# One decode step on one core: 32x32 block transposes on VectorE in place of TensorE transposes, wide matmuls, and loads in another order and in longer runs

## The chip, the core and the metric

The kernel runs on 1 core of one Trainium2 chip. The metric is the device time of one execution in microseconds (us), the median of several runs. The profile is that of one execution. Engines: PE is TensorE (PEld its weight loads), DVE is VectorE, ACT is ScalarE, POOL is GpSimd, SP is SyncE, which here only issues DMAs.

## The reference, cut to what matters

One token goes through an attention branch over a window of cached keys and values and through an MLP branch; both read the same normalised vector and both are added to x.

```python
W = min(4096, max(256, Sk // 4))          # 4096 of Sk = 65536
xn = _layernorm(A_x)                      # 1 x 1024, bf16
q = (xn @ wq)                             # wq 1024 x 4096: 32 heads of 128
k, v = last W rows of k_cache, v_cache    # 4 groups of 4096 x 128, 8 heads each
p = softmax(q k^T * 128 ** -0.5)
a = (p @ v) @ wo                          # wo 4096 x 1024
y = _layernorm(xn)
m = gelu(y @ w1 + b1) @ w2 + b2           # w1 1024 x 3584, w2 3584 x 1024
return A_x + a + m
```

All of it is read once: wq 8.4 MB, w1 7.3, K 4.2, V 4.2, w2 7.3, wo 8.4, together 39.8 MB.

## The kernel before, in words

Everything is placed by hand, with semaphores between the engines; there are no loops on the chip, so each engine runs its instructions in program order. SP issues all large loads, in this order: wq and w1 (line 139, `load_rows`), K (line 187), V (line 192), and, once h is computed (the wait at line 286 stands between), w2 and wo (line 139 again). Each load fills the 128 partitions; one run of a partition is as long as its share of the load, 16 KB for a chunk of two rows of wq, 8 KB for a group of K. w2 goes into the space of w1, wo into that of wq. wo's seven chunks (8, 8, 8, 4, 2, 1, 1 rows per partition) end with small ones. Small loads (x as a column, x and b2 as rows, b1 as columns) are issued by ACT; x as a column is 128 runs of 16 bytes.

- Normalisation: DVE, ACT and two small matmuls (lines 196 to 246) give XNTb (for q) and YTb (for h).
- q (`row_product`, line 255): for each of the 8 rows of wq in a partition, eight matmuls of 512 columns with a single weight column; q stands as one row in PSUM. DVE and ACT copy it out, 32 tiny matmuls (line 273) turn it into columns.
- h (line 255): the same with w1, seven matmuls a row; the copies are at lines 281 and 283, the 28 tiny transposes at line 305, bias and gelu at lines 310 to 326.
- K: 128 transposes of 128x128 on PE (line 344), copied from PSUM back into the K buffer by DVE (line 351) and ACT (line 356). Scores: 128 matmuls of 8 columns with a K block as weights (line 366).
- Softmax: maximum per head across partitions (lines 371 to 387), exponential on ACT (line 392), sums (line 395).
- P V: 128 matmuls of 128 columns (line 433), all of a group in one column group of the array. The result is divided by the sum (line 439) and folded into columns OT (lines 444, 448).
- Output: x and b2 (lines 418, 419), w2 and wo (`out_rows_mms`, line 409) accumulate into one PSUM bank; each row of a weight takes four matmuls of 256 columns, one for each of the four 32-column groups of the array. ACT copies the result (line 457), and ACT and SP store it in two halves.

The matmuls of line 409 wait chunk by chunk for the loads of w2 and wo.

Of the kernel before, what the change touches and what calls it, by code (L numbers as in the profile page):

```python
# [9 lines left out]
D = 1024  # L10
F = 3584
HQ = 32
HKV = 4
DH = 128
REP = HQ // HKV
SK = 65536
W = 4096
NBLK = W // 128
FC = F // 128
KC = D // 128  # L20
NQ = HQ * DH
WQ_CHUNKS = [2, 2, 2, 2]
W1_CHUNKS = [2, 2, 2, 2]
W2_CHUNKS = [9, 9, 8, 2]
WO_CHUNKS = [8, 8, 8, 4, 2, 1, 1]
PAD = 32
# [14 lines left out]
def bass_parallel_sum__sliding_block_cached__mixer_channel_mlp__decode_kernel(  # L41
# [23 lines left out]
    s_x, s_xrow, s_b1T, s_b2, s_out = (nc.alloc_semaphore(n) for n in ("s_x", "s_xrow", "s_b1T", "s_b2", "s_out"))  # L65
    s_out2 = nc.alloc_semaphore("s_out2")
# [16 lines left out]
    identb = sb("identb", [128, 128], bf16)  # L83
    identf = sb("identf", [128, 128], f32)
    onesf = sb("onesf", [128, 128], f32)
    E4 = sb("E4", [128, 4 * 128], bf16)
    XB = sb("XB", [128, KC], bf16)
    XBR = sb("XBR", [1, 2 * D], bf16)
# [8 lines left out]
    ROW = sb("ROW", [1, NQ], bf16)  # L97
    Qrow = ROW[:, 0:NQ]
    Hrow = ROW[:, 0:F]
    ORow = sb("ORow", [128, 256], bf16)  # L100
    QT = sb("QT", [128, HQ], bf16)
    B1T = sb("B1T", [128, FC], bf16)
    HT = sb("HT", [128, FC], f32)
    U2 = sb("U2", [128, FC], f32)
    GT = sb("GT", [128, FC + PAD], bf16)
    MXP = sb("MXP", [128, 32], f32)
    MX32 = sb("MX32", [32, 1], f32)
    DIAG = sb("DIAG", [32, 32], f32)
    NMB = sb("NMB", [128, 32], f32)
    Pb = sb("Pb", [128, HKV * NBLK * REP + PAD], bf16)  # L110
    SUMP = sb("SUMP", [128, 128], f32)
    REC = sb("REC", [128, 1], f32)
    ON = sb("ON", [128, DH], bf16)
    OT = sb("OT", [128, 32 + PAD], bf16)
    KV = sb("KV", [128, HKV * W + HKV * NBLK * DH], bf16)
    KT = KV[:, 0:HKV * W]
    V = KV[:, HKV * W: HKV * W + HKV * NBLK * DH]
    W1 = sb("W1", [128, KC * F], bf16)
    W2 = W1[:, 0:FC * D]
    WA = sb("WA", [128, KC * NQ], bf16)  # L120
# [15 lines left out]
    def load_rows(dst, src, chunks, width, semaphores):  # L136
        c0 = 0
        for j, n in enumerate(chunks):
            sp.dma_start(  # L139
                dst[:, c0 * width:(c0 + n) * width].rearrange("p (c n) -> p c n", c=n),  # L140
                src[:, c0:c0 + n, :],
            ).then_inc(semaphores[j], 16)
            c0 += n


    with nc.allow_non_contiguous_dma(reason="small loads"):
        act.dma_start(XB[:, :], x_col).then_inc(s_x, 16)
        act.dma_start(XBR[:, 0:D], x_row).then_inc(s_xrow, 16)
        act.dma_start(XBR[:, D:2 * D], b2_row).then_inc(s_b2, 16)
        act.dma_start(B1T[:, :], b1_T).then_inc(s_b1T, 16)  # L150

    C["onesf"] = POOL.mark(pool.memset(onesf[:, :], 1.0))
    POOL.mark(pool.memset(identb[:, :], 0.0))
    pool.wait_ge(POOL.sem, POOL.cnt)
    C["identb"] = POOL.mark(pool.affine_select(
        out=identb[:, :], in_=identb[:, :], pattern=[[-1, 128]], compare_op=ALU.not_equal,
        fill=1.0, base=0, channel_multiplier=1))
    POOL.mark(pool.memset(identf[:, :], 0.0))
    pool.wait_ge(POOL.sem, POOL.cnt)
    C["identf"] = POOL.mark(pool.affine_select(  # L160
        out=identf[:, :], in_=identf[:, :], pattern=[[-1, 128]], compare_op=ALU.not_equal,
        fill=1.0, base=0, channel_multiplier=1))
    POOL.mark(pool.memset(E4[:, :], 0.0))
    pool.wait_ge(POOL.sem, POOL.cnt)
    pool.wait_ge(POOL.sem, POOL.cnt)
    for g in range(HKV):

        POOL.mark(pool.affine_select(
            out=E4[32 * g:32 * g + REP, :].rearrange("p (q m) -> p q m", q=4),
            in_=E4[32 * g:32 * g + REP, :].rearrange("p (q m) -> p q m", q=4),  # L170
            pattern=[[1, 4], [-1, 128]], compare_op=ALU.not_equal, fill=1.0,
            base=32 * g, channel_multiplier=4))
        pool.wait_ge(POOL.sem, POOL.cnt)
    POOL.mark(pool.memset(SUMP[:, :], 1.0))
    pool.wait_ge(POOL.sem, POOL.cnt)
    POOL.mark(pool.memset(GT[:, FC:FC + PAD], 0.0))
    pool.wait_ge(POOL.sem, POOL.cnt)
    POOL.mark(pool.memset(OT[:, 32:32 + PAD], 0.0))
    pool.wait_ge(POOL.sem, POOL.cnt)
    POOL.mark(pool.memset(Pb[:, HKV * NBLK * REP:], 0.0))  # L180
    C["consts"] = POOL.cnt


    load_rows(WA, wq_p, WQ_CHUNKS, NQ, s_wq)
    load_rows(W1, w1_p, W1_CHUNKS, F, s_w1)
    for g in range(HKV):
        sp.dma_start(
            KT[:, g * W:(g + 1) * W],
            A_k_cache[0, g, SK - W:SK, :].rearrange("(m b) d -> m (b d)", m=128),
        ).then_inc(s_k[g], 16)  # L190
    for g in range(HKV):
        sp.dma_start(
            V[:, g * NBLK * DH:(g + 1) * NBLK * DH],
            A_v_cache[0, g, SK - W:SK, :].rearrange("(m b) d -> m (b d)", m=128),
        ).then_inc(s_v[g], 16)


    def stats(src, ms, veps):
        DVE.mark(dve.tensor_reduce(  # L199
            out=ms[:, 0:2], in_=PS[:, 7 * 512: 7 * 512 + 16].rearrange("p (a k) -> p a k", a=2),  # L200
            axis=AX.X, op=ALU.add))
        C["d_sum"] = DVE.cnt
        dve.wait_ge(DVE.sem, DVE.cnt)
        DVE.mark(dve.tensor_scalar(out=ms[:, 2:4], in0=ms[:, 0:2], scalar1=INV_D, scalar2=None, op0=ALU.mult))
        dve.wait_ge(DVE.sem, DVE.cnt)
        DVE.mark(dve.tensor_tensor(out=ms[:, 4:5], in0=ms[:, 2:3], in1=ms[:, 2:3], op=ALU.mult))
        dve.wait_ge(DVE.sem, DVE.cnt)
        C[veps] = DVE.mark(dve.scalar_tensor_tensor(
            out=ms[:, 5:6], in0=ms[:, 3:4], scalar=EPS, in1=ms[:, 4:5], op0=ALU.add, op1=ALU.subtract))

    dve.wait_ge(s_x, 16)
    DVE.mark(dve.tensor_copy(XT16[:, 0:8], XB[:, :]))
    dve.wait_ge(DVE.sem, DVE.cnt)
    C["xsq"] = DVE.mark(dve.tensor_tensor(out=XT16[:, 8:16], in0=XT16[:, 0:8], in1=XT16[:, 0:8], op=ALU.mult))  # L214

    pe.wait_ge(DVE.sem, C["xsq"])
    pe.wait_ge(POOL.sem, C["onesf"])
    C["sum1"] = PE.mark(pe.matmul(PS[:, 7 * 512: 7 * 512 + 16], lhsT=onesf[:, :], rhs=XT16[:, 0:16]))  # L218
    dve.wait_ge(PE.sem, C["sum1"])
    stats(XT16, msx, "veps1")  # L220
# [3 lines left out]
    DVE.mark(dve.reciprocal(out=msx[:, 7:8], in_=msx[:, 6:7]))  # L224
    dve.wait_ge(DVE.sem, DVE.cnt)
    DVE.mark(dve.tensor_scalar(out=XNT[:, :], in0=XT16[:, 0:8], scalar1=msx[:, 2:3], scalar2=msx[:, 7:8],  # L226
                               op0=ALU.subtract, op1=ALU.mult))
    dve.wait_ge(DVE.sem, DVE.cnt)
    C["xn"] = DVE.mark(dve.tensor_copy(XNTb[:, :], XNT[:, :]))
    dve.wait_ge(DVE.sem, DVE.cnt)  # L230
    DVE.mark(dve.tensor_copy(YT16[:, 0:8], XNTb[:, :]))  # L231
    dve.wait_ge(DVE.sem, DVE.cnt)
    C["ysq"] = DVE.mark(dve.tensor_tensor(out=YT16[:, 8:16], in0=YT16[:, 0:8], in1=YT16[:, 0:8], op=ALU.mult))
    pe.wait_ge(DVE.sem, C["ysq"])
    C["sum2"] = PE.mark(pe.matmul(PS[:, 7 * 512: 7 * 512 + 16], lhsT=onesf[:, :], rhs=YT16[:, 0:16]))  # L235
    dve.wait_ge(PE.sem, C["sum2"])
    stats(YT16, msy, "veps2")
# [5 lines left out]
    DVE.mark(dve.reciprocal(out=msy[:, 7:8], in_=msy[:, 6:7]))  # L243
    dve.wait_ge(DVE.sem, DVE.cnt)
    C["y"] = DVE.mark(dve.tensor_scalar(out=YTb[:, :], in0=YT16[:, 0:8], scalar1=msy[:, 2:3], scalar2=msy[:, 7:8],
                                        op0=ALU.subtract, op1=ALU.mult))


    def row_product(weights, chunks, width, semaphores, vec, tiles, name):
        k = 0  # L250
        for j, n in enumerate(chunks):
            pe.wait_ge(semaphores[j], 16)
            for _ in range(n):
                for t in range(tiles):
                    last = pe.matmul(  # L255
                        PS[0:1, t * 512:(t + 1) * 512], lhsT=vec[:, k:k + 1],
                        rhs=weights[:, k * width + t * 512: k * width + (t + 1) * 512],
                        start=(k == 0), stop=(k == KC - 1))
                k += 1
        C[name] = PE.mark(last)  # L260

    pe.wait_ge(DVE.sem, C["d_sum"])
    row_product(WA, WQ_CHUNKS, NQ, s_wq, XNTb, 8, "q")
    dve.wait_ge(PE.sem, C["q"])
    C["d_qrow"] = DVE.mark(dve.tensor_copy(Qrow[:, 0:2048], PS[0:1, 0:2048]))  # L265
# [228 lines left out]
```

## Time and profile before

| what | value |
|---|---|
| time before, median of 3 runs | 102.41 us (102.35 to 102.55) |
| span of the profiled execution, first to last instruction | 101.1 us |
| PE busy | 69.9 us (69%) |
| DVE busy | 21.4 us (21%) |
| ACT busy | 13.8 us (14%) |
| HBM read | 39.86 MB, 394 GB/s over the span |
| mean granted TensorE clock | 0.825 |

How to read the rows that follow. In a line of groups, after the engine and the operation come the tiles (out<-in), the shape, the count, then busy time and mean ns of one, then idle time just before and what ended it. In a timeline or a chain the first two columns are the start in us from the span's start and the duration. In a table of stretches the columns after the engines are the granted clock (1.00 is full speed), the share of time in which the DMA engines were busy, and GB/s; a packet is counted where it begins, so a share can pass 1.00. An engine named with q (SPq) is its DMA issues.

### The profile page before, as it was taken

What the parts mean: (1) busy time and instruction counts of PE and PEld (TensorE: products, weight loads), DVE (VectorE), ACT (ScalarE), POOL (GpSimd) and SP (SyncE); (2) the same over time, 40 slices, a digit from 0 to 9 for tenths busy, and PEclk for the clock granted to TensorE, in tenths of its full rate; (3) what the DMA queues carried; (4) which work ended last, traced back from release to release, by engine and by line L of the source; (5) the groups of instructions that cost most, each with busy time, mean ns of one, the idle gap of its engine ahead of it and who ended that gap; (6) DMA issues with size and microseconds to landing.
All of it is one profiled execution on the core that took longest, in us unless ns stands there. A gap on an engine that the chain in (4) does not pass through costs nothing.

```text
span 101.1 us, 1804 instructions
## 1 busy us (share of the span) xinstructions
PE 69.9 (69%) x825; PEld 42.9 (42%) x825; DVE 21.4 (21%) x46; ACT 13.8 (14%) x16; POOL 4.8 (5%) x18
## 2 busy tenths in 40 slices
PE   0002299999955999998599986556999944070780
PEld 0001232333314223332599975244999833040420
DVE  0003530000045000001885953456000100000000
ACT  0400060000042000001563750040000000000001
POOL 6740000000000000000000000000000000000000
PEclk9999999999997558999999998555559999555555
DMA  4899999999999999999999999999999999999920
GB/s 97 363 441 405 442 428 421 415 441 420 442 431 414 432 431 401 421 418 421 415 431 421 415 454 422 445 408 424 424 394 462 421 421 428 421 418 399 398 101 1
DMA packets 4194, 39.96 MB, mean 395 GB/s; under 512 B 726, under 2 KB 730, under 8 KB 1244
## 3 DMA queue, kind: packets, MB, share of 16 engines
q1 hardware_dynamic: 3892, 39.85, 94.0%
q8 instruction: 6, 0.10, 0.4%
q10 hardware_dynamic: 296, 0.01, 0.2%
HBM read 39.86 MB, written 0.00 MB: 394 GB/s over the span
## 4 chain that ended last, share of the span: by engine, by line
DMA 38%; PE 34%; SPq 20%; DVE 5%; issue 1%; ACT 1%
PE PS L255 31%; DMA WA<-in_A_wo_dram 30%; SPq L139 20%; DMA XB<-in_A_x_dram 8%; DVE ROW L265 2%; PE PS L273 1%; PE PS L218 1%; PE PS L235 1%; PE PS L409 0%; ACT ORow L457 0%; DVE XNT L226 0%; ACT msx L222 0%; DVE msx L199 0%; DVE msy L199 0%; DVE YT L231 0%
## 5 line engine op out<-in xcount | busy, mean ns | idle before, releaser
L255 PE MATMUL PS<-WA,XNTb 128*1 128x512 bf16 x64 | 16.7, 429 | 0.3 <-DVE msy L199 0.3
L255 PE MATMUL PS<-W,YTb 128*1 128x512 bf16 x56 | 15.2, 441 | 0.0
L409 PE MATMUL PS<-WA,OT 128*32 128x256 bf16 x128 | 7.3, 379 | 9.3 <-DMA WA<-in_A_wo_dram 9.3
L255 PEld LDWEIGHTS PS<-WA,XNTb 128*1 128x1 bf16 x64 | 5.8, 92 | 10.7 <-issue 3.9
L433 PE MATMUL PS<-KV,Pb 128*32 128x128 bf16 x128 | 9.3, 261 | 0.0
L409 PEld LDWEIGHTS PS<-WA,OT 128*32 128x32 bf16 x128 | 3.8, 123 | 12.9 <-DMA WA<-in_A_wo_dram 10.3
L255 PEld LDWEIGHTS PS<-W,YTb 128*1 128x1 bf16 x56 | 5.2, 94 | 9.5 <-issue 4.2
L433 PEld LDWEIGHTS PS<-KV,Pb 128*32 128x32 bf16 x128 | 9.2, 120 | 0.0
L344 PE MATMUL PS<-identb,KV 128*128 128x128 bf16 x128 | 7.5, 219 | 1.5 <-ACT ROW L281 1.5
L344 PEld LDWEIGHTS PS<-identb,KV 128*128 128x128 bf16 x128 | 7.2, 98 | 2.1 <-ACT ROW L281 2.0
L218 PE MATMUL PS<-XT,onesf 128*128 128x16 f32 x2 | 0.6, 386 | 8.8 <-DVE XT L214 8.8
L351 DVE COPY KV<-PS 128x1024 bf16<-128x1024 bf16 x10 | 6.3, 683 | 0.7 <-PE PS L344 0.7
L356 ACT ACTIVATE KV<-PS 128x1024 bf16<-128x1024 bf16 x6 | 5.8, 1018 | 1.9 <-PE PS L344 1.9
L265 DVE CAST ROW<-PS 1x2048 bf16<-1x2048 f32 x1 | 2.3, 2279 | 15.4 <-PE PS L255 15.4
L409 PE MATMUL PS<-W,GT 128*32 128x256 bf16 x112 | 4.8, 320 | 1.1 <-DMA W<-in_B_w_dram 1.1
L283 DVE CAST ROW<-PS 1x2048 bf16<-1x2048 f32 x1 | 2.3, 2279 | 14.9 <-PE PS L255 14.9
L457 ACT ACTIVATE ORow<-PS 128x256 bf16<-128x256 f32 x1 | 0.4, 383 | 31.0 <-PE PS L409 31.0
L409 PEld LDWEIGHTS PS<-W,GT 128*32 128x32 bf16 x112 | 3.5, 111 | 1.8 <-DVE PS L387 1.6
L218 PEld LDWEIGHTS PS<-XT,onesf 128*128 128x128 f32 x2 | 0.5, 313 | 8.8 <-DVE XT L214 8.8
L267 ACT ACTIVATE ROW<-PS 1x2048 bf16<-1x2048 f32 x1 | 1.9, 1866 | 14.4 <-PE PS L255 14.4
L281 ACT ACTIVATE ROW<-PS 1x1536 bf16<-1x1536 f32 x1 | 1.4, 1439 | 16.6 <-PE PS L255 16.6
L366 PE MATMUL PS<-QT,KV 128*128 128x8 bf16 x128 | 3.4, 166 | 0.4 <-DVE KV L351 0.4
(75 smaller groups left out, 34.5 us busy)
## 6 DMA issues: line engine op xcount, KB each, us to landing
WA<-in_A_wq_dram SPq DMA_DIRECT2D x4, 2048.0 KB, 14.2
W<-in_B_w_dram SPq DMA_DIRECT2D x4, 1792.0 KB, 29.9
WA<-in_A_wo_dram SPq DMA_DIRECT2D x3, 2048.0 KB, 38.4
W<-in_B_w_dram SPq DMA_DIRECT2D x2, 2304.0 KB, 21.6
KV<-in_A_k_cache_dram SPq DMA_DIRECT2D x4, 1024.0 KB, 39.3
KV<-in_A_v_cache_dram SPq DMA_DIRECT2D x4, 1024.0 KB, 34.1
W<-in_B_w_dram SPq DMA_DIRECT2D x1, 2048.0 KB, 28.8
WA<-in_A_wo_dram SPq DMA_DIRECT2D x1, 1024.0 KB, 42.3
```

The lines of the kernel that those rows point to most:

```text
L139: sp.dma_start(dst[:, c0 * width:(c0 + n) * width].rearrange("p (c n) -> p c n", c=n), src[:, c0:c0 + n, :],).then_inc(semaphores[j], 16)
L218: C["sum1"] = PE.mark(pe.matmul(PS[:, 7 * 512: 7 * 512 + 16], lhsT=onesf[:, :], rhs=XT16[:, 0:16]))
L255: last = pe.matmul(PS[0:1, t * 512:(t + 1) * 512], lhsT=vec[:, k:k + 1], rhs=weights[:, k * width + t * 512: k * width + (t + 1) * 512], s ...
L265: C["d_qrow"] = DVE.mark(dve.tensor_copy(Qrow[:, 0:2048], PS[0:1, 0:2048]))
L267: C["a_qrow"] = ACT.mark(act.activation(out=Qrow[:, 2048:4096], in_=PS[0:1, 2048:4096], func=ACTF.Copy))
L283: C["d_hrow"] = DVE.mark(dve.tensor_copy(Hrow[:, 1536:F], PS[0:1, 1536:F]))
L344: last = pe.matmul(PSb[:, o:o + 128], lhsT=KT[:, col + bb * 128: col + (bb + 1) * 128], rhs=identb[:, :], is_transpose=True)
L351: C["dkt"][u] = DVE.mark(dve.tensor_copy(KT[:, col + 1024 * s: col + 1024 * (s + 1)], PSb[:, bk * 1024:(bk + 1) * 1024]))
L356: C["akt"][u] = ACT.mark(act.activation(out=KT[:, col + 1024: col + 2048], in_=PSb[:, bk * 1024:(bk + 1) * 1024], func=ACTF.Copy))
L366: last = pe.matmul(PS[:, g * 256 + b * 8: g * 256 + (b + 1) * 8], lhsT=KT[:, g * W + b * 128: g * W + (b + 1) * 128], rhs=QT[:, g * 8:(g + ...
L409: ins = pe.matmul(acc(a), lhsT=vec[:, c:c + 32], rhs=weights[:, c * D + a * 256: c * D + (a + 1) * 256], start=False, stop=(c == stop_at))
L433: last = pe.matmul(PS[32 * g:32 * g + 32, 4 * 512:4 * 512 + DH], lhsT=Pb[:, i * REP:i * REP + 32], rhs=V[:, i * DH:(i + 1) * DH], start=(b ...
```

## The change

- Loads. wq and w1 come in two chunks of four rows instead of four of two, w2 in chunks of 18 and 10 rows (before 9, 9, 8, 2), wo in 16, 8, 4, 2, 1, 1 (before 8, 8, 8, 4, 2, 1, 1). The order is wq, K, w1, V; w2 follows when q is computed, into wq's space; wo follows when h is computed, its rows 0 to 27 into w1's space and 28 to 31 into K's. x, b2 and b1 are loaded as four rows each, onto partitions 0, 32, 64 and 96 (b2: 1, 33, 65, 97).
- q and h: four matmuls of 512 (448) columns for the four column groups, the weight column broadcast to 32 columns; the results lie on four blocks of 32 equal partitions. DVE transposes 32x32 blocks (`dve.transpose`) to turn x, q, h and P into columns; four matmuls with a selection matrix SELQ and four copies build QB, q in a block-diagonal form.
- K: four transposes in place on DVE, 128x4096 each; scores in 32 matmuls of 512 columns with QB as weights. P: one transpose and 16 copies.
- P V: 32 matmuls of 512 columns over all four groups at once, taking turns on the column groups; a mask GMASK keeps each head's own group.
- Output: w2 and rows 0 to 27 of wo in two matmuls of 512 columns a row with one weight column (`bulk`), on two column groups in one PSUM bank; x, b2 and rows 28 to 31 in four matmuls of 256 columns in another. DVE copies the first bank in four pieces (BULK) and adds it to the second; SP stores the result in one DMA.

The diff, cut to its core (added lines alone where a whole part is new):

```diff
-WQ_CHUNKS = [2, 2, 2, 2]
-W1_CHUNKS = [2, 2, 2, 2]
-W2_CHUNKS = [9, 9, 8, 2]
-WO_CHUNKS = [8, 8, 8, 4, 2, 1, 1]
+WQ_CHUNKS = [4, 4]
+W1_CHUNKS = [4, 4]
+W2_CHUNKS = [18, 10]
+WO_CHUNKS = [16, 8, 4, 2, 1, 1]
+WO_BULK = 28
...
     load_rows(WA, wq_p, WQ_CHUNKS, NQ, s_wq)
-    load_rows(W1, w1_p, W1_CHUNKS, F, s_w1)
     for g in range(HKV):
         sp.dma_start(
             KT[:, g * W:(g + 1) * W],
...
+    load_rows(W1, w1_p, W1_CHUNKS, F, s_w1)
     for g in range(HKV):
         sp.dma_start(
...
+        act.dma_start(XB4[0:128:32, :], x_rows).then_inc(s_x, 16)
+        act.dma_start(XB4[1:128:32, :], b2_rows).then_inc(s_b2, 16)
+        act.dma_start(B1R[0:128:32, :], b1_rows).then_inc(s_b1, 16)
...
+    def wide_product(weights, chunks, width, semaphores, vec, n, banks, name):
+        k = 0
+        for j, rows in enumerate(chunks):
+            pe.wait_ge(semaphores[j], 16)
+            for _ in range(rows):
+                for b in range(2):
+                    for a in range(4):
+                        lo = k * width + (2 * a + b) * n
+                        last = pe.matmul(
+                            PS[32 * a:32 * a + 32, banks[b] * 512: banks[b] * 512 + n],
+                            lhsT=vec[:, k:k + 1].to_broadcast([128, 32]), rhs=weights[:, lo:lo + n],
+                            start=(k == 0), stop=(k == KC - 1))
+                k += 1
+        C[name] = PE.mark(last)
+
+    wide_product(WA, WQ_CHUNKS, NQ, s_wq, XNTb, 512, [0, 1], "q")
+
+    sp.wait_ge(PE.sem, C["q"])
+    load_rows(WA, w2_p, W2_CHUNKS, D, s_w2)
...
+    C["TQ"] = d(dve.transpose(TQ[:, :], Q4[:, :]))
...
+    for g in range(HKV):
+        dve.wait_ge(s_k[g], 16)
+        C["kt"].append(d(dve.transpose(KT[:, g * W:(g + 1) * W], KT[:, g * W:(g + 1) * W])))
...
+        for hb in range(2):
+            for c in range(4):
+                last = pe.matmul(
+                    PS[32 * g:32 * g + 32, hb * 512:(hb + 1) * 512],
+                    lhsT=QB[:, (g * 4 + c) * 32:(g * 4 + c + 1) * 32], rhs=kg[:, c, 16 * hb:16 * hb + 16, :],
+                    start=(c == 0), stop=(c == 3))
...
+    d(dve.transpose(PT1[:, :], Pb[:, :]))
+    dw()
+    for g in range(HKV):
+        for a in range(4):
+            C["PT"] = d(dve.tensor_copy(
...
+    wide_product(W1, W1_CHUNKS, F, s_w1, YTb, QW // 2, [4, 5], "h")
+    sp.wait_ge(PE.sem, C["h"])
+    load_rows(W1, wo_p, WO_CHUNKS[:3], D, s_wo[:3])
+    load_rows(KT, wo_p, WO_CHUNKS[3:], D, s_wo[3:], first=WO_BULK)
...
+    for b in range(NB):
+        q = b % 4
+        last = pe.matmul(PS[32 * q:32 * q + 32, 3 * 512:4 * 512], lhsT=PT[:, b * 32:(b + 1) * 32], rhs=vb[:, b],
+                         start=(b < 4), stop=(b >= NB - 4))
...
+    def bulk(weights, vec, c, lo, first, last):
+        for q in range(2):
+            ins = pe.matmul(PS[32 * q:32 * q + 1, 6 * 512:7 * 512], lhsT=vec[:, c:c + 1],
+                            rhs=weights[:, lo + q * 512: lo + (q + 1) * 512], start=first, stop=last)
+        return ins
...
+            if c < WO_BULK:
+                last = bulk(W1, OT, c, c * D, False, c == WO_BULK - 1)
...
+            else:
+                for a in range(4):
+                    lo = (c - WO_BULK) * D + a * 256
+                    last = pe.matmul(PS[32 * a:32 * a + 32, 7 * 512:7 * 512 + 256],
+                                     lhsT=OT[:, c:c + 1].to_broadcast([128, 32]), rhs=KT[:, lo:lo + 256],
+                                     start=False, stop=(c == 31))
...
+    dve.wait_ge(PE.sem, C["bulk"])
+    for a in range(4):
+        q = a // 2
+        lo = 6 * 512 + (a % 2) * 256
+        d(dve.tensor_copy(BULK[32 * a:32 * a + 1, :], PS[32 * q:32 * q + 1, lo:lo + 256]))
+    dw()
+    dve.wait_ge(PE.sem, C["fin"])
+    C["out"] = d(dve.tensor_tensor(out=ORow[:, :], in0=bank(7, 0, 256), in1=BULK[:, :], op=ALU.add))
+    sp.wait_ge(DVE.sem, C["out"])
+    sp.dma_start(out_rows, ORow[0:128:32, :]).then_inc(s_out, 16)
```

More of the change, by code (lines that the diff above doesn't have):

```diff
@@ new lines, in bulk @@
+    def bulk(weights, vec, c, lo, first, last):
[3 more added lines that the diff above has]
+        return ins
+    pe.wait_ge(DVE.sem, C["GT"])
+    c = 0
+    for j, n in enumerate(W2_CHUNKS):
+        pe.wait_ge(s_w2[j], 16)
+        for _ in range(n):
+            bulk(WA, GT, c, c * D, c == 0, False)
+            c += 1
```

515 lines of the change are left out of this document (232 added, 283 removed).

## The prediction

> **What bounds the kernel now.** I read the page first (engines, DMA slices, queues), then the chain of waits in order of time, then busy time in stretches near the end, then the timeline of TensorE.
>
> ```profile
> span 101.1 us, 1804 instructions
> ...
> PE 69.9 (69%) x825; PEld 42.9 (42%) x825; DVE 21.4 (21%) x46; ACT 13.8 (14%) x16; POOL 4.8 (5%) x18
> ...
> DMA  4899999999999999999999999999999999999920
> ...
> DMA packets 4194, 39.96 MB, mean 395 GB/s; under 512 B 726, under 2 KB 730, under 8 KB 1244
> q1 hardware_dynamic: 3892, 39.85, 94.0%
> q8 instruction: 6, 0.10, 0.4%
> q10 hardware_dynamic: 296, 0.01, 0.2%
> ```
>
> The DMA engines are full from the second slice to the 38th. Queue q1 (the loads issued by SP) takes 94.0% of 16 engines' span: 95.1 us of 101.1. The bytes are the same after the change, so only three things can move the end: what a byte costs on the DMA engines, a hole in their stream, and the work behind the last landing.
>
> ```profile
> 0.73 7.63 DMA XB<-in_A_x_dram
> ...
> 67.91 30.42 DMA WA<-in_A_wo_dram
> 98.34 0.04 issue
> 98.38 0.43 PE PS L409 x4
> ...
> 98.84 0.38 ACT ORow L457
> ```
>
> The chain ends with the last row of wo: landed at 98.34, multiplied by 98.8, copied by 99.2, then the store. The chain names TensorE and SP earlier (lines 255 and 139), but the DMA slices are full there too: SP was only late with issues that stood far back in a full queue. So shorter TensorE stages are worth nothing by themselves.
>
> ```profile
> 78.00:91.00 13.00, 7.07 (x178) 5.45 (x172) 0.54 (x2) 0.00 (x0) 0.00 (x0) 0.82 1.01 425
> ...
> 95.00:96.00 1.00, 0.40 (x12) 0.14 (x8) 0.00 (x0) 0.00 (x0) 0.00 (x0) 0.50 1.00 385
> 96.00:97.00 1.00, 0.89 (x16) 0.32 (x8) 0.00 (x0) 0.00 (x0) 0.00 (x0) 0.50 0.50 188
> 97.00:98.00 1.00, 0.89 (x12) 0.25 (x12) 0.00 (x0) 0.00 (x0) 0.00 (x0) 0.50 0.27 100
> ```
>
> The last three columns are granted clock, DMA share and GB/s. Full engines move 425 GB/s in long runs (16 KB a partition) and 385 GB/s in 2 KB runs. Half of the engines are done by about 96.5, the last at about 98.
>
> **The change, part by part.** Times are positions in the profiled span of 101.1 us; the median of the runs shown, 102.41, lies 1.3 us above it, and I keep that distance.
>
> *Longer runs.* One engine moves 425/16 = 26.6 bytes/ns in 16 KB runs and 385/16 = 24.1 in 2 KB runs: 617 and 85 ns a run. The difference, 532 ns for 14,336 bytes, gives 26.9 bytes/ns and a fixed 9 ns a run. Before, the 27 large loads have 128 runs each, 8 for each engine: 216. After there are 20 loads (2 wq, 4 K, 2 w1, 4 V, 2 w2, 6 wo): 160. That saves 56 x 9 = 0.50 us. Each load also ends in one small completion packet per engine; they fit the count, 27 x (128 + 16) = 3888 of the 3892 packets of q1. Seven fewer at no more than 9 ns: 0.06 us. Bounds: 0, if runs above 16 KB are cut up again, and 0.6.
>
> *Small loads.* x and b1 go from 128 short runs each to 4 rows each. Queue q10 falls from 0.2% of the span to nearly nothing: 0.2 us per engine (0.15 to 0.25 by the rounding). The x load's 7.63 us at the start shrink too, but then q waits for wq: no gain.
>
> By the Trainium skill (DMA: Bandwidth & Descriptors, Anatomy of one DMA) each DMA carries about 2.0 us of fixed cost; seven fewer would then give 14 us if it stood in the stream. The trace disagrees: the share is 1.01 across many loads, so that cost is overlapped, and the sum doesn't take it.
>
> *Sum for the stream:* 0.50 + 0.06 + 0.20 = 0.76; the last landing comes at 98.34 - 0.76 = 97.58, if no hole opens.
>
> *Holes.* SP issues w2 behind q and wo behind h, past K and V, now issued earlier.
>
> ```profile
> 17.55 15.48 SPq L192 DMA_DIRECT2D KV<-in_A_v_cache_dram  x4
> ...
> 99.25 0.60 SPq L461 DMA_DIRECT2D out_dram<-ORow  x1
> ```
>
> SP got its last V load out at 33.0, when about 31 us x 425 GB/s = 13.2 of 24.1 MB had moved: some 11 MB can stand in the queue. By 425 GB/s from 2 us, wq has landed at 22, K at 32, w1 at 49, V at 59, w2 at 76. w2 must be issued by 59 and wo by 76.
>
> ```profile
> 12.53 16.66 PE L255 MATMUL PS<-WA,XNTb 128*1 128x512 bf16 x64 [0.27 <-DVE msy L199]
> ...
> 12.91 0.13 PEld L255 LDWEIGHTS PS<-WA,XNTb 128*1 128x1 bf16 x1 [0.30 <-issue]
> ...
> 17.60 0.13 PEld L255 LDWEIGHTS PS<-WA,XNTb 128*1 128x1 bf16 x1 [0.30 <-issue]
> 18.01 10.66 PEld L255 LDWEIGHTS PS<-WA,XNTb 128*1 128x1 bf16 x50 [0.29 <-issue]
> ...
> 32.52 15.17 PE L255 MATMUL PS<-W,YTb 128*1 128x512 bf16 x56
> ...
> 38.45 8.73 PEld L255 LDWEIGHTS PS<-W,YTb 128*1 128x1 bf16 x41 [0.30 <-issue]
> ...
> 62.33 1.23 DVE L371 TENSOR_REDUCE MXP<-PS 128x32 f32<-128x1024 f32 x1 [2.85 <-PE PS L366]
> ...
> 66.80 1.02 ACT L392 ACTIVATE Pb<-PS 128x1024 bf16<-128x1024 f32 x1 [7.20 <-DVE PS L387]
> ...
> 80.84 1.27 PE L409 MATMUL PS<-W,GT 128*32 128x256 bf16 x40
> ```
>
> From 12.91 to 17.60 are 12 loads, 0.427 us apart: 512 columns at half clock. From 18.01 on it is 10.66/50 = 0.213. Four column groups do overlap: 40 matmuls of 256 columns in 1.27 us are 32 ns each, where one alone would need 107. So the q product, 16 steps of four, has 8 steps left when wq ends: 22 + 8 x 0.427 = 25.8, and w2 follows at once. Copies, transposes and selection of q I put at 3.5 us, so the K transposes start at about 29.
>
> ```profile
> L351 DVE COPY KV<-PS 128x1024 bf16<-128x1024 bf16 x10 | 6.3, 683 | 0.7 <-PE PS L344 0.7
> L265 DVE CAST ROW<-PS 1x2048 bf16<-1x2048 f32 x1 | 2.3, 2279 | 15.4 <-PE PS L255 15.4
> L395 DVE TENSOR_REDUCE SUMP<-Pb 128x32 f32<-128x1024 bf16 x1 | 2.0, 1971 | 1.1 <-ACT Pb L392 1.1
> L387 DVE TENSOR_TENSOR PS<-PS,NMB 128x1024 f32<-128x1024 f32 x1 | 1.2, 1233 | 0.0
> ```
>
> No row shows a VectorE transpose. For 4096 elements a partition the nearest rows bound it: four times 0.683 = 2.7 us and four times 1.971 = 7.9. I take four times L387's 1.233, one element a step: 4.9. (The Trainium skill, VectorE: DVE Perf Modes, The three transpose paths, has 311 ns for 128x128; no run here shows it.) Four of them end at 29 + 20 = 49; the last group's 8 score matmuls, all in one column group, 3.4: 52; maximum to exponential, 5.5 before (62.33 to 67.82): 58; h, 16 steps of 448 columns at half clock, 6: 64. wo is issued 12 us ahead of 76. P's transpose and 16 small copies at most 0.45 each, P V in 8 steps of 0.427 and the output's fold give OT at about 72. Nothing there ends late.
>
> *The end.* w2 and wo now use two column groups of 512 instead of four of 256: 0.427 us a row at half clock, 0.213 at full, twice as much as before. Rows 0 to 15 of wo are one load.
>
> ```profile
> 88.47 1.90 PE L409 MATMUL PS<-WA,OT 128*32 128x256 bf16 x32 [3.75 <-DMA WA<-in_A_wo_dram]
> 93.36 1.90 PE L409 MATMUL PS<-WA,OT 128*32 128x256 bf16 x32 [2.99 <-DMA WA<-in_A_wo_dram]
> 95.85 1.04 PE L409 MATMUL PS<-WA,OT 128*32 128x256 bf16 x16 [0.60 <-DMA WA<-in_A_wo_dram]
> ```
>
> These are rows 8 to 15, 16 to 23 and 24 to 27; relative to the last landing (98.34), 9.87, 4.98 and 2.49 us earlier. Today each finishes before the next lands. After, 16 rows become ready 9.87 ahead, on a TensorE idle for some 5 us and at half clock (here too: 1.90 against 1.27 for 40). The q product came to full clock 5.5 us after its start (12.5 to 18.0), h 5.9 (32.5 to 38.45). With 5.7: 13.3 rows slow, the other 14.7 of 28 at 0.213 = 3.1; done 9.87 - 5.7 - 3.1 = 1.05 ahead, 0.9 with the last one's latency. Then four copies of 1x256 into BULK: from L265 and L387, 1.02 ns an element and 0.19 fixed, so 0.45 each, 1.65 with the overlap of L351's copies (6.3 us for ten of 0.683). The final add starts 0.8 after the landing, where the output copy now starts 0.5 after; the add is 0.45 against 0.38. Together +0.38. Bounds: full clock at once gives -0.1; half clock throughout ends the 28 rows 2.3 after the landing, +3.5.
>
> The Trainium skill (TensorE: Matmul & The Clock Gate, Part 1) speaks against this edit: after an idle window the clock is halved until a free-running window of 3.4 us was busy, so 3.4 to 6.8 us from the start. The trace agrees (5.5 and 5.9). By that rule alone, as an estimate, the end would vary from 101.5 to 102.6 between executions.
>
> *Sum:* 101.1 - 0.76 + 0.38 = 100.7 in the span, 102.41 - 0.38 = 102.0 as a median.
>
> **The rivals.**
> - *Faster: the engines finish together.* The stretches from 96 to 98 show some engines 1.5 us behind. q8's six code packets cost 0.4% of 16 x 101.1 us, 1.08 us each: about that lag. TensorE's instructions fall from 825 matmuls to some 340, so two or three fetches remain. If late engines catch 0.5 us or the clock comes early, 101.4. Against: one late engine suffices.
> - *The long runs don't pay.* Cut at 16 KB again, they save only 0.26: 102.5. For: no row shows a run above 18 KB.
> - *Slower: TensorE's backlog on wo.* Its price is that of the end above: it decides from the point at which row 27 is done later than 1.2 us before the last landing, which the forecast already passes; a slow clock for over 7 us gives 102.7, for the whole 105.1. For: the clock is 0.50 in every stretch after 95. Against: 6.8 us of unbroken matmuls, longer than both measured warm-ups.
> - *Slower: late transposes.* At L395's price the middle moves by 12 us, OT comes at 84, 56 rows take 5.7 + 42.7 x 0.213 = 14.8 and the end slips 1.7: 103.7. Decides above about 7.5 us a transpose. If the two column groups did not overlap, about 107.
>
> **How the numbers follow.** Forecast 102.0: 0.50, of which 0.08 lies within 0.2% of 102.41. Engines together or early clock, 101.4: 0.18. Long runs don't pay, 102.5: 0.12. Backlog, 102.7 to 105.1: 0.14. Late transposes or no overlap: 0.06. About 0.2% is what a measurement of this kernel can tell from no change. Faster 0.42 + 0.18 = 0.60; same 0.08 + 0.12 = 0.20; slower 0.20. The range 101.2 to 103.0 leaves out under 0.05 below and about 0.12 above.
>
> **What would show it.** Right: DMA slices full without a break to the 37th or 38th; q1 near 2,900 packets at about 93.5%, q10 near 0; SP's wo issues well before 75; the last wo landing 0.6 to 0.9 earlier; the BULK copies ending within 1 us of it. Wrong: a gap in the DMA slices; a K transpose above 7 us; q1's share unchanged; TensorE still in rows 0 to 27 when row 31 has landed; several us between the last landing and the store.

## The result, and the profile after

The changed kernel takes 101.72 us (median; 101.42 to 103.07 over 20 runs), the kernel before, run beside it, 102.52 (102.31 to 102.89, 20 runs). The ratio is 0.9933, with a 95% interval of 0.9914 to 0.9951: faster by 0.67%, more than the 0.2% that a measurement can tell. A run more than 1.5% above the fastest of its kernel, here the one of 103.07, counts as slow and is left out of the ratios. The forecast was 102.0 against 102.41, a gain of 0.4 us; the gain is 0.8, twice as much.

The profiled execution of the changed kernel took 102.1 us, in the slower third of its runs. From its page: the span, busy time by engine, the granted clock and the DMA share in 40 slices, and the queues.

```profile
span 100.7 us, 870 instructions
...
PE 45.9 (46%) x346; PEld 17.6 (17%) x346; DVE 43.2 (43%) x73; ACT 5.2 (5%) x9; POOL 7.9 (8%) x31
...
PEclk9999999975555555699999579997558995555998
DMA  7699999979999998998999998999999999999910
...
DMA packets 2915, 39.90 MB, mean 396 GB/s; under 512 B 336, under 2 KB 352, under 8 KB 736
...
q1 hardware_dynamic: 2888, 39.85, 93.6%
q8 instruction: 2, 0.03, 0.1%
q10 hardware_dynamic: 24, 0.01, 0.0%
```

TensorE works a third less and VectorE twice as long, and neither is what the time follows: the DMA slices are full to the 38th, as before. The time that the packets take, over all queues, falls from 94.6% of 101.1 us (95.6 us an engine) to 93.7% of 100.7 (94.4).

The chain that ended last, in order of time (start, duration, what):

```profile
1.26 21.70 DMA WA<-in_A_wq_dram
...
32.14 17.43 DVE KT L312 x4
...
60.68 27.11 DMA W<-in_A_wo_dram
87.80 0.14 issue
87.93 8.81 PE PS L446 x56
96.75 0.02 issue
96.77 0.41 DVE BULK L479
...
98.11 0.43 DVE BULK L479
98.54 0.02 issue
98.57 0.42 DVE ORow L482
```

Before, the chain ended with the landing of the last row of wo. Now its last link to a DMA is the landing of wo's first chunk, at 87.80, and the 11 us behind that are TensorE and VectorE. The last row is hidden beside them, as the timeline shows (idle time and its end in brackets):

```profile
87.93 8.79 PE L446 MATMUL PS<-W,OT 128*1 128x512 bf16 x56 [7.34 <-DMA W<-in_A_wo_dram]
...
92.58 0.13 PEld L446 LDWEIGHTS PS<-W,OT 128*1 128x1 bf16 x2 [0.30 <-issue]
93.01 0.13 PEld L446 LDWEIGHTS PS<-W,OT 128*1 128x1 bf16 x2 [0.30 <-issue]
93.33 2.89 PEld L446 LDWEIGHTS PS<-W,OT 128*1 128x1 bf16 x28 [0.18 <-issue]
...
96.77 1.76 DVE L479 COPY BULK<-PS 1x256 f32<-1x256 f32 x4 [26.29 <-PE PS L446]
...
97.77 0.29 PE L469 MATMUL PS<-KT,OT 128*32 128x256 bf16 x4 [0.34 <-DMA KT<-in_A_wo_dram]
98.57 0.42 DVE L482 TENSOR_TENSOR ORow<-PS,BULK 128x256 bf16<-128x256 f32 x1
```

The last row landed just ahead of 97.77, 0.6 us earlier than the 98.34 before. Its product was done at 98.06, and the final add had to wait another half microsecond for the four copies into BULK. They were late because rows 0 to 27 ran at half clock (a pair of weight loads for each row, 0.43 us apart) until 93.3.

The trace's record of the granted clock says when it can change. In this execution it changes at 18.11, 21.53, 42.01, 55.66, 59.07, 69.31, 76.14, 82.97 and 93.21 us, always a whole multiple of 3.41 us apart. wo's rows start at 87.93, between two points of that grid (86.38 and 89.80), and the clock comes one whole step after the second. In the other profiles below the steps are the same, but the grid lies elsewhere (68.38, 75.20, 88.86 and 95.68 in the one with wo in seven chunks). So how long after its start a burst of matmuls gets the full clock depends, as far as these profiles show, on where the grid lies in that execution.

### The profile page after: what moved, and what is told of

Read it like the earlier page. It is cut to its first block, busy times and chain, and to the rows that moved or that the text cites. A ratio compares the mean times of both kernels' runs of the same rounds, so it can differ in the third digit from the quotient of the medians.

```text
span 100.7 us, 870 instructions
## 1 busy us (share of the span) xinstructions
PE 45.9 (46%) x346; PEld 17.6 (17%) x346; DVE 43.2 (43%) x73; ACT 5.2 (5%) x9; POOL 7.9 (8%) x31
## 4 chain that ended last, share of the span: by engine, by line
DMA 48%; DVE 26%; PE 20%; ACT 1%; issue 1%; SPq 0%; DVEq 0%
DMA W<-in_A_wo_dram 27%; DMA WA<-in_A_wq_dram 22%; DVE KT L312 17%; PE PS L446 9%; PE PS L278 8%; DVE QB L305 3%; PE PS L320 2%; DVE BULK L479 2%; DVE TQ L296 1%; DVE MX L328 1%; ACT Pb L348 1%; DVE Q L291 1%; DVE ORow L482 0%; PE PS L300 0%; PE PS L341 0%
## 5 line engine op out<-in xcount | busy, mean ns | idle before, releaser
L312 DVE STREAM_TRANSPOSE KT<-KT 128x4096 bf16<-128x4096 bf16 x4 | 17.4, 4413 | 0.0
L320 PE MATMUL PS<-KT,QB 128*32 128x512 bf16 x32 | 9.8, 460 | 12.6 <-DVE KT L312 12.6
L446 PE MATMUL PS<-W,OT 128*1 128x512 bf16 x56 | 8.8, 489 | 7.3 <-DMA W<-in_A_wo_dram 7.3
L446 PE MATMUL PS<-WA,GT 128*1 128x512 bf16 x56 | 8.5, 468 | 1.6 <-DMA WA<-in_B_w_dram 1.6
L278 PE MATMUL PS<-WA,XNTb 128*32 128x512 bf16 x64 | 6.9, 608 | 4.4 <-DMA WA<-in_A_wq_dram 4.4
L320 PEld LDWEIGHTS PS<-KT,QB 128*32 128x32 bf16 x32 | 3.2, 110 | 18.8 <-DVE KT L312 14.6
L446 PEld LDWEIGHTS PS<-W,OT 128*1 128x1 bf16 x56 | 2.9, 102 | 13.2 <-issue 11.5
L278 PE MATMUL PS<-W,YTb 128*32 128x448 bf16 x64 | 4.8, 473 | 0.0
L355 DVE COPY TQ<-Q 32x256 bf16<-32x256 bf16 x16 | 3.5, 219 | 0.5
L305 DVE CAST QB<-PS 32x128 bf16<-32x128 f32 x4 | 2.8, 709 | 0.6 <-PE PS L300 0.5
## 6 DMA issues: line engine op xcount, KB each, us to landing
KT<-in_A_k_cache_dram SPq DMA_DIRECT2D x4, 1024.0 KB, 26.6
```

The costliest lines, as they stand in the source:

```text
L278: last = pe.matmul(PS[32 * a:32 * a + 32, banks[b] * 512: banks[b] * 512 + n], lhsT=vec[:, k:k + 1].to_broadcast([128, 32]), rhs=weights[: ...
L305: C["QB"] = d(dve.tensor_copy(QB[32 * a:32 * a + 32, :].rearrange("p (g c a h) -> p a g h c", g=4, c=4, a=4)[:, a], PS[32 * a:32 * a + 32, ...
L312: C["kt"].append(d(dve.transpose(KT[:, g * W:(g + 1) * W], KT[:, g * W:(g + 1) * W])))
L320: last = pe.matmul(PS[32 * g:32 * g + 32, hb * 512:(hb + 1) * 512], lhsT=QB[:, (g * 4 + c) * 32:(g * 4 + c + 1) * 32], rhs=kg[:, c, 16 * h ...
L355: C["PT"] = d(dve.tensor_copy(PT[32 * a:32 * a + 32, :].rearrange("p (b m) -> p b m", b=NB)[:, :, 8 * g:8 * g + 8], PT1[32 * g:32 * g + 32 ...
L446: ins = pe.matmul(PS[32 * q:32 * q + 1, 6 * 512:7 * 512], lhsT=vec[:, c:c + 1], rhs=weights[:, lo + q * 512: lo + (q + 1) * 512], start=fi ...
```

## The experiments

The theory (A in the texts below) has three parts: the gain lies in the DMA stream (fewer runs, fewer small packets); the middle of the kernel, with K's transposes on VectorE, has slack to spare; the end gives part of the gain back, by as much as the clock comes late. The rivals are in each text: that the piece tried is worth nothing, that it works the other way, or that code fetches count. Ratios are to the kernel before, run beside each kernel.

**The old, shorter loads of wq, w1 and w2 in the changed kernel.**

```diff
-WQ_CHUNKS = [4, 4]
-W1_CHUNKS = [4, 4]
-W2_CHUNKS = [18, 10]
+WQ_CHUNKS = [2, 2, 2, 2]
+W1_CHUNKS = [2, 2, 2, 2]
+W2_CHUNKS = [9, 9, 8, 2]
```

> The changed kernel with wq, w1 and w2 in the old chunks (2, 2, 2, 2; 2, 2, 2, 2; 9, 9, 8, 2), so in the old run lengths; the order, the chunks of wo and all else as changed. Theory A (a run costs each DMA engine 9 ns whatever its length, so longer runs shorten the stream): 48 more runs on each engine, 0.43 us, and 6 more completions, 0.05: q1 near 3,750 packets, the last landing about 0.5 us later than the 97.7 of the changed kernel's profile, median 102.2. Theory B (the runs' length is worth nothing; the gain is elsewhere): 101.7 and the last landing at 97.7.

Measured 102.07 us (101.82 to 102.26), ratio 0.9955 (0.9939 to 0.9971), 0.35 slower than the changed kernel's median. q1 carries 3,752 packets, as expected; the last row landed at about 97.9, 0.2 us later than in the changed kernel's profile, not 0.5. The runs are worth something, but the changed end is in this figure, and it spreads by more than the effect. The experiments on the four-group version below repeat it without that.

**wo in seven chunks, as before, in the changed kernel** (the first four of them, not three, now go into w1's space).

```diff
-WO_CHUNKS = [16, 8, 4, 2, 1, 1]
+WO_CHUNKS = [8, 8, 8, 4, 2, 1, 1]
```

> The changed kernel with wo in the old chunks (8, 8, 8, 4, 2, 1, 1): the first 16 rows come as two loads. Theory A (what the end costs is the time at which TensorE's clock goes up): 8 rows at half clock are 3.4 us of every 4.9, so no full window is busy, the clock stays at half, row 27 is done 0.3 us after the last landing and not 1.0 before, the copies and the add follow late: 102.6 to 103.1. Theory B (what it costs is the backlog of 16 rows that land at once): the backlog is halved, row 27 is done earlier: 101.3 to 101.5.

Measured 102.34 us, anywhere from 101.47 to 103.13 over 12 runs; ratio 0.9982 (0.9956 to 1.0007). That smaller chunks would clear the end falls. That they make it worse holds in direction, with a median 0.3 below the low end that was expected. The spans say it more clearly: ten of the 12 lie at 100.9 to 101.3 us, where half of the changed kernel's 20 are at 100.3 or less. The reason expected, a clock that stays at half, doesn't hold in the profiled execution (102.16 us):

```profile
87.86 0.95 PEld L446 LDWEIGHTS PS<-W,OT 128*1 128x1 bf16 x12 [3.42 <-DMA W<-in_A_wo_dram]
87.86 2.65 PE L446 MATMUL PS<-W,OT 128*1 128x512 bf16 x16 [2.92 <-DMA W<-in_A_wo_dram]
89.02 0.14 PEld L446 LDWEIGHTS PS<-W,OT 128*1 128x1 bf16 x2 [0.20 <-issue]
89.44 0.14 PEld L446 LDWEIGHTS PS<-W,OT 128*1 128x1 bf16 x2 [0.29 <-issue]
...
92.75 3.97 PE L446 MATMUL PS<-W,OT 128*1 128x512 bf16 x22 [2.24 <-DMA W<-in_A_wo_dram]
```

Eight rows take 2.65 us, where half clock throughout would need 3.4 and full clock 1.7. They start at full clock, kept from the rows before, and lose it on the way: the granted clock is 1.00 from 75.2 to 88.9 and 0.50 from there to 95.7. The next eleven rows take 3.97, between 4.7 and 2.35, because the clock comes back only at 95.7, at their end. So short bursts with pauses between them can keep the clock or lose it, and here it was gone when the last big chunk landed.

**TensorE kept busy: 30 matmuls of 512 columns, their results dropped, ahead of wo.**

```diff
     pe.wait_ge(DVE.sem, C["OT"])
+    for _ in range(30):
+        pe.matmul(PS[0:1, 0:512], lhsT=GT[:, 0:1], rhs=WA[:, 0:512], start=True, stop=True)
```

> The changed kernel with 30 matmuls of 512 columns more between the last row of w2 and the first of wo; their result goes to an unused bank and is dropped. Theory A (the clock): TensorE is at full clock when wo's first 16 rows land, they take 3.4 us, row 27 is done soon after its own landing, 1.4 before the last: median 101.3 to 101.5, and the spread of the runs shrinks from 1.6 us to under 0.5. Theory B (the end costs the same whatever the clock, for example by the copies): 101.7 and the same spread; slower if 30 matmuls are too many.

Measured 101.50 us (101.48 to 101.50), ratio 0.9906 (0.9893 to 0.9920). Of the spread of the changed kernel (1.65 us over 20 runs, spans of 100.1 to 101.0) nothing is left in these four runs (spans of 100.2), though TensorE has more to do. The timeline of its end:

```profile
87.70 3.62 PE L446 MATMUL PS<-W,OT 128*1 128x512 bf16 x32 [0.78 <-DMA W<-in_A_wo_dram]
...
92.59 1.89 PE L446 MATMUL PS<-W,OT 128*1 128x512 bf16 x16 [1.28 <-DMA W<-in_A_wo_dram]
...
95.08 1.03 PE L446 MATMUL PS<-W,OT 128*1 128x512 bf16 x8 [0.59 <-DMA W<-in_A_wo_dram]
96.15 1.76 DVE L481 COPY BULK<-PS 1x256 f32<-1x256 f32 x4 [25.34 <-PE PS L446]
...
97.62 0.29 PE L471 MATMUL PS<-KT,OT 128*32 128x256 bf16 x4 [0.34 <-DMA KT<-in_A_wo_dram]
```

Sixteen rows take 3.62 us: full clock from the first. Each chunk is done before the next lands, BULK is ready at 97.91, and the last row's product, at 97.94, is what ends last. From the last landing (97.57) to the end of the add it is 0.88 us, as long as the end of before takes. So what the changed kernel's end pays for is the clock, not the copies as such.

**The old end in the changed kernel:** all output rows in four matmuls of 256 columns on four column groups, in one bank; no BULK, no add; ACT copies the result. The store stays a single DMA, issued by SP.

```diff
-        for q in range(2):
-            ins = pe.matmul(PS[32 * q:32 * q + 1, 6 * 512:7 * 512], lhsT=vec[:, c:c + 1],
-                            rhs=weights[:, lo + q * 512: lo + (q + 1) * 512], start=first, stop=last)
+        for a in range(4):
+            ins = pe.matmul(PS[32 * a:32 * a + 32, 7 * 512:7 * 512 + 256],
+                            lhsT=vec[:, c:c + 1].to_broadcast([128, 32]),
+                            rhs=weights[:, lo + a * 256: lo + (a + 1) * 256], start=False, stop=False)
...
-    C["out"] = d(dve.tensor_tensor(out=ORow[:, :], in0=bank(7, 0, 256), in1=BULK[:, :], op=ALU.add))
+    C["out"] = ACT.mark(act.activation(out=ORow[:, :], in_=bank(7, 0, 256), func=ACTF.Copy))
```

> The changed kernel with the output products as before the change: four matmuls of 256 columns a row on the four column groups, all in one bank, no copies into BULK, ACT copies the result. All else as changed. Theory A (stream shorter by 0.6 us, spoilt at the end by two slow column groups and four copies): the copy to the output starts 0.5 us after the last landing whatever the clock: 101.3, spread under 0.5. Theory B (the end is not what varies): 101.7, with the spread of the changed kernel.

Measured 101.45 us (101.30 to 101.64), ratio 0.9903 (0.9887 to 0.9919): no version here is faster, and it is ahead of both kernels. Its chain ends as that of before did, with the last row's landing, now at 97.44:

```profile
62.33 35.11 DMA KT<-in_A_wo_dram
97.44 0.04 issue
97.48 0.43 PE PS L470 x4
97.91 0.02 issue
97.94 0.38 ACT ORow L477
```

From landing to the end of the copy it is 0.88 us, as before (98.34 to 99.22). Not all of its gain of 1.0 us is in the stream, though. The kernel before stored its result in two halves, this one and the changed kernel in one DMA (first before, then here):

```profile
99.25 0.60 SPq L461 DMA_DIRECT2D out_dram<-ORow  x1
99.25 0.58 ACTq L459 DMA_DIRECT2D out_dram<-ORow  x1
```

```profile
98.34 0.62 SPq L479 DMA_DIRECT2D out_dram<-ORow  x1
```

From the issue of the store to the end of the span are 1.9 us in both profiles with two stores (before, and before with the new chunks) and 1.7 in all twelve with one. So 0.2 us of the gain is the store's, and some 0.8 is in the stream; no run changed the store alone. This version is the base on which the stream's parts can be weighed without the end. Adding the 30 dropped matmuls to it as well changes nothing:

> The kernel with the output in four column groups and, in addition, the 30 matmuls ahead of wo whose result is dropped. If the clock still matters at its end, only the last four matmuls get shorter (0.43 us at half clock, 0.32 at full): 101.3 to 101.4. If not: 101.45.

Measured 101.47 us (101.41 to 101.53), ratio 0.9902 (0.9888 to 0.9917). The clock is back at half by the last rows (the last product takes 0.40 us, not 0.29), and four groups don't need it.

**The runs, on the four-group version:** all the old chunks of wq, w1, w2 and wo. And the converse: the kernel before with the new chunks and nothing else.

```diff
-WQ_CHUNKS = [4, 4]
-W1_CHUNKS = [4, 4]
-W2_CHUNKS = [18, 10]
-WO_CHUNKS = [16, 8, 4, 2, 1, 1]
+WQ_CHUNKS = [2, 2, 2, 2]
+W1_CHUNKS = [2, 2, 2, 2]
+W2_CHUNKS = [9, 9, 8, 2]
+WO_CHUNKS = [8, 8, 8, 4, 2, 1, 1]
```

> The kernel with the output in four column groups (101.45 us, last landing at 97.4), which has no clock-dependent end, with all chunks of wq, w1, w2 and wo as before the change: 56 more runs and 7 more completions on each engine. Theory A (9 ns a run): +0.50 to +0.56, 101.95 to 102.0, the last landing near 98.0. Theory B (run lengths worth nothing): 101.45.

> The kernel before with the new chunks of wq, w1, w2 and wo alone: 216 runs on each engine become 160, 27 loads become 20. Theory A: -0.56, 101.9, with q and h some 5 us later (the short runs of x now alternate with runs of 32 KB) and hidden. Theory B (run lengths worth nothing): 102.45.

Measured 101.91 us (101.81 to 102.05), ratio 0.9946 (0.9932 to 0.9959) for the first, and 102.04 (101.91 to 102.16), ratio 0.9959 (0.9945 to 0.9972) for the second. Short runs cost the one 0.46 us, long runs gain the other 0.47: the same figure from both sides, and about 8 ns for each of the 56 runs of an engine, their seven completion packets included. The queue rows, first with short runs, then the kernel before with long ones:

```profile
q1 hardware_dynamic: 3896, 39.85, 94.5%
```

```profile
q1 hardware_dynamic: 2884, 39.85, 93.9%
```

Packets fall with the runs, so a run of 32 or 36 KB goes as one packet and isn't cut up again.

**The small loads, on the four-group version:** the old column loads of x and b1, of 128 short runs each, come in addition and go into buffers that nothing reads.

```diff
+        act.dma_start(DX[:, :], A_x.rearrange("b s (p r) -> (b s p) r", r=KC)).then_inc(s_dx, 16)
+        act.dma_start(DB[:, :], B_b1.rearrange("(p c) -> p c", c=FC)).then_inc(s_db, 16)
```

> The kernel with the output in four column groups, with the two loads of 128 short runs of before (x as a column, b1 as columns) issued in addition, into unused buffers. Theory A (they cost the stream 0.2 us of each engine): 101.65. Theory B (a small run goes between large ones at no cost): 101.45.

Measured 101.63 us (101.47 to 101.92), ratio 0.9923 (0.9908 to 0.9938): 0.18 slower (the intervals of the two versions overlap), as their share of the engines' time says:

```profile
q10 hardware_dynamic: 312, 0.02, 0.2%
```

**The order, on the four-group version:** w1 ahead of K again.

```diff
     load_rows(WA, wq_p, WQ_CHUNKS, NQ, s_wq)
+    load_rows(W1, w1_p, W1_CHUNKS, F, s_w1)
     for g in range(HKV):
...
-    load_rows(W1, w1_p, W1_CHUNKS, F, s_w1)
```

> The kernel with the output in four column groups, with w1 loaded ahead of K as before the change. The K transposes then start some 10 us later and the middle ends at about 80 instead of 70. Theory A (all of the middle is hidden, what counts is the stream): 101.45, within 0.15. Theory B (the order, with K's transposes early, is part of the gain): above 102.

Measured 101.45 us (101.34 to 101.60), ratio 0.9903 (0.9890 to 0.9917): the order of the loads is worth nothing here.

**More code, on the four-group version:** waits on a semaphore that has long been reached, 2,500 in the source, which stand as 1,250 more instructions in the trace.

```diff
     C["consts"] = POOL.cnt
+    for _ in range(1200):
+        pool.wait_ge(s_wq[0], 16)
...
+    for _ in range(500):
+        sp.wait_ge(s_wq[0], 16)
     sp.wait_ge(PE.sem, C["h"])
...
+    for _ in range(800):
+        act.wait_ge(s_wq[0], 16)
     act.wait_ge(PE.sem, C["fin"])
```

> The kernel with the output in four column groups, with 1,250 instructions more, all waits that are long fulfilled: 600 on POOL behind its constants, 400 on ACT ahead of the last copy, 250 on SP ahead of the wait for h. They hold nothing up, but are 64 bytes each, 80 KB of code or five more fetches of 16 KB on q8. Theory C (each fetch holds one DMA engine for about 1.06 us, and the fewer fetches of the changed kernel, 2 or 3 in place of 6, are the rest of the gain): q8 at 7 to 9, the mean engine 0.33 us later, the last landing 0.3 to 0.7 later, 101.75 to 102.1. Theory D (the rest is something else): 101.45.

Measured 103.31 us (103.24 to 103.38), ratio 1.0082 (1.0070 to 1.0094): 1.9 us slower, far more than either theory gave it, and the packets came on q14 and not, as expected, on q8. Nothing new of any length stands on the chain, which still ends with the last row, landing at 99.36. Its queues, then its windows (DMA share and GB/s in the last two columns), then those of the four-group version without the waits:

```profile
q14 instruction: 11, 0.09, 0.2%
q8 instruction: 3, 0.05, 0.2%
```

```profile
96.00:97.00 1.00, 0.41 (x12) 0.05 (x8) 0.00 (x0) 0.00 (x0) 0.00 (x0) 0.50 0.42 164
97.00:98.00 1.00, 1.00 (x16) 0.42 (x16) 0.00 (x0) 0.00 (x0) 0.00 (x0) 0.50 0.13 49
98.00:99.00 1.00, 0.85 (x12) 0.25 (x12) 0.00 (x0) 0.00 (x0) 0.00 (x0) 0.50 0.06 23
```

```profile
96.00:97.00 1.00, 0.75 (x12) 0.25 (x12) 0.00 (x0) 0.00 (x0) 0.00 (x0) 0.50 0.21 80
97.00:98.00 1.00, 0.66 (x8) 0.11 (x4) 0.00 (x0) 0.06 (x1) 0.00 (x0) 0.50 0.00 0
98.00:99.00 1.00, 0.00 (x0) 0.00 (x0) 0.00 (x0) 0.32 (x1) 0.00 (x0) 0.50 0.00 0
```

Ten more code packets on q14 are all that is added to the DMA engines, some 3 us of one engine's time together (0.2% of 16 x 102 us). Spread evenly that is 0.2 us an engine. But from 97 to 98 two engines of 16 still work (0.13), and from 98 to 99 one (0.06). So fetches of code can delay the end of a full stream. That the packets fell on few engines, and that the last row waits for the latest of them, is inferred: the trace doesn't name the engine of a packet. A single fetch more need not cost anything: with the 30 dropped matmuls q8 carries four code packets of 16 KB, without them three, and the times are the same (101.47 and 101.45). How much of the gain comes from the two to four fetches that the changed versions have fewer on q8 was not measured apart: a version with the changed kernel's loads and the old code was not tried.

**Slower transposes:** the first group of K transposed three times in place of once (8.8 us more on VectorE; three transposes leave the data as one does), then the first two groups (17.6 more).

```diff
         dve.wait_ge(s_k[g], 16)
+        for _ in range(2 if g < 1 else 0):
+            d(dve.transpose(KT[:, g * W:(g + 1) * W], KT[:, g * W:(g + 1) * W]))
+            dw()
```

> The changed kernel with the first group of K transposed three times in place of once (twice more gives back the same), 8.8 us more on VectorE ahead of the scores. Theory A (the middle is hidden, the clock decides the end): OT comes at 79, TensorE goes through w2 and wo in one run and is at full clock when wo's last rows land: 101.4 to 101.6 with a spread under 0.5, faster than the changed kernel. Rival (VectorE's transposes are on the path): up to 8.8 us slower.

> The changed kernel with the first two groups of K transposed three times, 17.6 us more on VectorE. Theory A (slack of the middle about 10 us): OT comes at 88, TensorE starts w2 at 89 and needs 14.8 us for the 56 rows of w2 and wo: the end slips by 7 to 8 us, 108.5 to 109.5, though the DMA stream has only a short hole. Rival (the middle has more slack, or TensorE catches up): under 105.

Measured 101.59 us (101.39 to 102.27), ratio 0.9927 (0.9900 to 0.9953) for one group. For two, the six runs go from 106.35 to 110.01 (median 108.45); the fastest, which is the profiled one, is 3.8 us above the kernel before, and what makes the others longer is not shown. The first 8.8 us cost nothing, and TensorE is at full clock when wo lands, as expected: the first sixteen rows take 3.62 us here too. The spread, 0.9 us, is more than was expected, but not the spans: all six are 100.1 to 100.3. The next 8.8 cost 5 in the fastest run.

In the profile of that run the DMA slices and SP's issue of wo's first loads show why:

```profile
DMA  6999999979999999897999998999809999999800
GB/s 200 387 412 400 402 412 499 474 296 427 424 421 466 447 404 469 371 502 340 427 421 430 560 413 365 421 430 405 354 8 399 399 399 418 418 424 405 327 10 1
```

```profile
78.05 1.28 SPq L146 DMA_DIRECT2D W<-in_A_wo_dram  x3
```

h is computed behind the scores, wo waits for h, and at 78.05 the queue had run dry: one slice of 2.6 us at 8 GB/s. OT was ready only at 87, so that w2's and wo's rows ran one behind the other to 101.1, and the copies into BULK and the add, to 103.4, came behind them.

## Why the prediction was right, and where it was off

*Bound: the stream.* Right. With four column groups the time moves with what the stream carries (runs, small loads, code) and not with the order of the loads, and two versions that give TensorE or VectorE more work (30 dropped matmuls, 8.8 us of transposes) are no slower than the changed kernel.

*Longer runs, 0.50 with 0.06 for completions.* Right in mechanism and nearly in size: 0.46 and 0.47 for both, where 0.56 was said. (The 2.0 us for each DMA that the prediction cites from the Trainium skill, DMA: Bandwidth & Descriptors, Anatomy of one DMA, is given there for DMAs issued by GpSimd; here SP issues the loads, and seven loads with 56 runs fewer gave 0.46 us, not 14.)

*Small loads, 0.20.* Right: 0.18, within what such small samples can tell.

*The x load "shrinks too".* Wrong, and harmless. The first transpose waited until 10.84 for x and b2, where x had landed at 8.36 before. q's first half started at 15.29 instead of 12.5 and was done at 18.6, 4 us ahead of the second half's landing at 22.96.

*The sum for the stream, 0.76.* Near, a little small. The four-group version gains about 1.05 against the kernel before; without the store's 0.2 the stream gave some 0.85. Runs and small loads are 0.65 of that, and no experiment assigns the other 0.2. The rival "the engines finish together" has code fetches for it, six on q8 before and two to four after: the experiment with more code shows that fetches can act this way, the equal times with three and four of them speak against one fetch counting, and the cause stays open. That the versions with a quiet end (four groups, or TensorE kept busy) reach that rival's 101.4 (101.45 and 101.50) doesn't show that the engines finish together: a quiet end and the store's 0.2 bring them most of the way. In the profiled execution of the changed kernel the last landing moved by 0.6, less than the sum, while in the four-group version it moved by 0.9: executions differ here by some tenths.

*The store.* This step is missing. The sum has nothing for one store in place of two, and gives no reason; the profiles show 0.2 us.

*Holes: none.* Right. wo was issued at 60.7, predicted 64, with 76 as the limit; the kernel with 17.6 us more transposes issued it at 78.05 and got the hole.

*The K transposes, 4.9 us each.* Right side of the bounds, a little high. The row, by line:

```profile
L312 DVE STREAM_TRANSPOSE KT<-KT 128x4096 bf16<-128x4096 bf16 x4 | 17.4, 4413 | 0.0
```

4.41 us for 4096 elements a partition, 1.08 ns each. (The Trainium skill's 311 ns for a 128x128 block, in VectorE: DVE Perf Modes, The three transpose paths, would give, as an estimate, 10 us for 32 of them; in one long instruction a block costs 138 ns.) They started at 32.1, not 29: q ended at 26.6, and the steps behind it took 5.5 us instead of 3.5, of which the four copies into QB are 2.9. (The prediction's 22 + 8 x 0.427 is 25.4, not 25.8; its 29 goes with 25.4.) The last scores were done at 51.5 (52 forecast), the exponential at 55.5 (58), h at 60.6 (64), OT at 70.5 (72).

*The late-transposes rival*, deciding above 7.5 us each, so some 12 us in all above what they take: inside what the two experiments bracket, 8.8 and 17.6. Its price did not see that wo's issue would pass its limit of 76 at nearly the same point; that is why 17.6 us more cost 4.9 even in the fastest run (106.35 against the 101.45 of a quiet end).

*The end, +0.38.* Right step by step in this execution: full clock 5.4 us after the start (5.7 taken), row 27 done 1.0 us before the last landing (0.9), the four copies 1.77 (1.65), the final add 0.84 after the landing (0.8). The median gives back less: 101.72 is 0.22 to 0.27 above the versions with a quiet end, as half of the executions have spans of 100.3 or less, like those with a quiet end. Over the 20 runs the spans go from 100.1 to 101.0 us, that is 101.4 to 102.3 with the usual 1.3 us between span and time. The Trainium skill (TensorE: Matmul & The Clock Gate, Part 1) has a free-running window of 3.4 us, from which the prediction worked out, as an estimate, full clock 3.4 to 6.8 us after the start and times of 101.5 to 102.6. The runs agree: the changes of the granted clock lie on a grid of 3.41 us, and the spread of the spans is within 0.1 us of that range.

*TensorE's backlog*, at 102.7 and above. Not seen. Two of the 20 runs are that long, 102.78 and 103.07, but their spans are 100.5 and 100.4, shorter than that of the profiled execution (100.7). What makes them long lies outside the stretch from the first to the last instruction, and it stays open; such runs are there in four versions with the changed end (up to 2.7 us between span and time) and in none with the old one.

*Why the total came out.* Three terms were off, all to the same side: the stream gave some 0.85 instead of 0.76, the store 0.2 instead of nothing, and the end took back 0.25 (to 101.72) instead of 0.38. Together that is a gain of 0.8 where 0.4 was said. The time lies well inside the range; the gain was forecast at half its size.

## What to carry to other kernels

When the DMA engines are full from start to end, count what each engine carries (runs, small packets, code fetches), look for the engine that finishes last, not at the mean, and price what stands behind the last landing, the store included; work moved between TensorE and VectorE is worth nothing until it delays an issue. Behind the last landing, take the form that is fast at half clock (here four column groups, 101.45 us) rather than the one that needs fewer instructions, or keep TensorE busy until the rows land. A median hides a spread: the changed kernel's fastest run, 101.42, is as fast as the best version, and when the clock comes decides how often. Compare spans as well as times: they tell a late clock from a delay outside the program's instructions.

## What the runs showed that was not expected

- A small load waits longer beside long runs. When x (and b2) could first be read, us from the start: as a column, 8.36 beside runs of 16 KB and 13.08 beside runs of 32 KB (the kernel before, and with the new chunks); as four rows, 8.2 beside 16 KB and 10.4 to 10.8 beside 32 KB. That fits small packets that take turns with the packets of wq on each engine; no view of the trace shows the turns themselves.
- 1,250 instructions that do nothing cost 1.9 us. All that they add to the DMA engines is ten code packets of 8 KB; that these fell on few engines is inferred.
- With 30 useless matmuls the spread was 0.02 us in four runs, against 1.65 in 20, and the median 0.2 us lower.
- One store in place of two took 0.2 us off the end.
